# W_tok loaded first by casting loads, and the order of all queues replayed from a table

## The chip, the core and the metric

The kernel runs on one core of a Trainium2 chip. The core has four engines that compute: TensorE (PE; its weight loads are listed apart as PEld), VectorE (DVE), ScalarE (ACT) and GpSimd (POOL). Each works through its own queue of instructions in order, and semaphores tie the queues together. SyncE (SP) only issues data transfers (DMAs); POOL issues some as well. All DMAs share 16 DMA engines. The metric is the time of one execution on the device, in microseconds (us).

## The reference

Inputs are q, k, v of shape (8 batches, 8 heads, 576, 64), a norm vector g of 64, a token-mixing matrix W_tok (576 x 576), W_ch1 (512 x 2048), W_ch2 (2048 x 512) and five vectors of 512.

```python
kv  = einsum('bhsd,bhse->bhde', k, v)           # attention without a softmax
o   = einsum('bhsd,bhde->bhse', q, kv)
x   = o / sqrt(mean(o*o, -1) + 1e-6) * g        # heads joined: (8, 576, 512)
tok = einsum('ts,bsd->btd', W_tok, alpha1 * x + beta1)
u   = x + lam * tok
ch  = relu((alpha2 * u + beta2) @ W_ch1) @ W_ch2
out = u + lam * ch
```

## The kernel before, in words

The 576 tokens of a batch are four chunks of 128 and a tail of 64; the tails of an even and an odd batch share one tile of 128 rows. For each batch the stages are:

- **kv** (L749, L755; for batch 0 `kv_first`, L725): the products of k and v, in f32.
- **norm** (L843; for batch 0 `norm_half`, L864): q times kv, then the mean square by an ACT square (L807) and a DVE reduction (L810), a square root (L813), a reciprocal (L816), and products that give x (L828) and r, which is x scaled for the token mix (L831).
- **tok** (L914; for batch 0 `tok_half`, L929; tails L948): W_tok transposed times r, five matmuls to a group, the fifth over the tail of 64 tokens. beta1's part enters through this fifth chunk: the tile wt holds, beside W_tok's last 64 rows, rows with W_tok's row sums (`wsums`, L1103 to L1113), which meet lam * beta1 in the tile rtl. DVE adds the result to x (L921; L937 for batch 0).
- **a2**: alpha2 * u + beta2 in bf16 and transposed. Batch 0 does it with TensorE transposes (`a2_pair`, L968) and ACT copies (L972). The others use two POOL operations per chunk (L986, L989) and a transposing DMA (L993).
- **ch1** and **ch2** (L1002, L1031; tails L1014): the channel mix, bf16 matmuls of 512 columns, with relu on ACT (L997). Then lam times the result (L1058), the addition (L1063) and the store.

The first channel-mix matmul of batch 0 (L1002) ends what is called the head below. In the head, batch 0 is done in two halves of the heads (j = 0, 1): pairs of heads of q, k and v are loaded by SP (`load_pair`, L611), q is rearranged by POOL (L698) and transposed by TensorE in f32 (`qt_early`, L703), and so on to a2. W_tok is loaded by SP in f32 (L629, L631), transposed by TensorE in f32 (L1081, L1084) and copied to bf16 by ACT (L1087, L1092). "Fillers" are matmuls on a constant tile (L597) whose results nobody uses. The weights W_ch1 and W_ch2 are loaded by POOL with a cast to bf16 (L1163, L1169), k and v of later batches also by POOL (L1186, L1190), q of later batches by SP in pieces of 128 bytes (L1178).

The order of the work is not that of the Python text. Every operation is recorded with what it reads and writes (`Prog.op`, `dma`, `mm`); `schedule` then plays the recorded operations through estimated costs, due times (`t0`, `pace`), shifts of single operations (`shift`) and extra waits (`gate`), puts out one sequence, and chooses the PSUM banks. A unit of that sequence is one operation or two TensorE operations woven together, matmul by matmul. Where TensorE has nothing to do in the head, `schedule` puts in fillers.

Of the kernel before, what the change touches and what calls it, by code (L numbers as in the profile page):

```python
# [9 lines left out]
BF16 = mybir.dt.bfloat16  # L10
# [8 lines left out]
DM = 512  # L19
# [4 lines left out]

class Op:


    __slots__ = ("bias", "q", "kind", "cost", "lat", "fns", "pri", "idx", "deps", "raw", "alloc",
                 "tiles", "start", "end", "pos", "waits", "inc", "clock", "slot", "nbytes",
                 "val", "margin", "tag", "narrow", "urgent", "ns")  # L30

    def __init__(self, q, kind, cost, lat, fns, pri, idx):
        self.q, self.kind, self.cost, self.lat = q, kind, cost, lat
        self.fns, self.pri, self.idx = fns, pri, idx
        self.deps, self.raw = set(), set()
        self.alloc, self.tiles = [], []
        self.start = self.end = self.pos = None
        self.waits, self.inc, self.clock = [], False, None
        self.slot = self.nbytes = self.val = self.ns = None
        self.margin = 0.0  # L40
        self.tag, self.narrow, self.urgent = "", False, False
# [12 lines left out]
class Prog:  # L54
    ENGINES = ("PE", "ACT", "DVE", "POOL")

    def __init__(self, nc, stack):
# [7 lines left out]
        self.main, self.fill = [], []  # L65
        self.bias = 0.0
        self.reach = 24
        self.warm, self.began, self.early, self.lead = 6.0, False, 45.0, 100.0
        self.t0, self.pace, self.last, self.shift = 31.0, 1.28, None, {}
        self.gate = {}  # L70
# [4 lines left out]
    def _add(self, o, r, w, after):  # L75
# [10 lines left out]
        for key in w:  # L86
# [5 lines left out]
            for y in self.readers.get(key, ()):  # L92
                if y is not o:
                    o.deps.add(y)
                    if not isinstance(key, Bank) and key[0] == "sm":
                        o.raw.add(y)
# [11 lines left out]
    def op(self, q, cost, fn, r=(), w=(), pri=0.0, lat=0.15, after=()):  # L108
        o = Op(q, "c", cost, lat, [fn], self.bias + pri, len(self.ops))
        o.bias = self.bias  # L110
        return self._add(o, r, w, after)

    def dma(self, q, slot, nbytes, fn, r=(), w=(), pri=0.0, after=(), issue=0.55):
        o = Op(q, "d", issue, 0.0, [fn], self.bias + pri, len(self.ops))
        o.slot = slot
        o.nbytes, o.ns = nbytes if isinstance(nbytes, tuple) else (nbytes, 20.0)
        o.bias = self.bias
        return self._add(o, r, w, after)

    def mm(self, stream, cols, fns, r=(), w=(), slow=False, after=(), margin=0.3,  # L120
           urgent=False):

        n = len(fns)
        per = cols * MM_NS + 0.0025
        each = slow if isinstance(slow, float) else {"r": 0.213}.get(slow, 0.109)
        o = Op("PE", "w" if slow and each is not slow else "m",
               n * (max(per, each) if slow else max(per, 0.056)),
               0.24, fns, self.bias, len(self.ops))
        o.bias = self.bias
        o.margin, o.narrow, o.urgent = 0.0 if urgent else margin, cols < 512, urgent  # L130
        (self.main if stream == "main" else self.fill).append(o)
        return self._add(o, r, w, after)


    def schedule(self):
        for i, j in self.gate.items():
            self.ops[i].deps.add(self.ops[j])
        due, t = {}, self.t0
# [1195 lines left out]
```

## Time and profile before

| | us |
|---|---|
| three runs | 354.62, 355.60, 358.28 |
| median | 355.60 |
| span of the profiled execution | 354.8 |
| TensorE busy | 341.3 |
| VectorE busy | 189.8 |
| GpSimd busy | 161.4 |
| ScalarE busy | 149.0 |

The span runs from the first to the last instruction of the profiled execution; the page gives no other time of that execution, so the span is used as its time. It lies between the runs' lowest time and their median. TensorE's matmuls are pipelined: the time from the start of one to the start of the next says more than the length of one. In rows of the timeline the first two numbers are the start and the length in us; in rows of groups the number behind the count is the total busy time, the next the mean in ns, then the idle time before them and what ended it.

### The profile page before, as it was taken

Reading aid. Unit: us, or ns where it says so; the run is one execution under the profiler, and the core shown is the slowest. Engines: PE = TensorE matmul, PEld = TensorE weight load, DVE = VectorE, ACT = ScalarE, POOL = GpSimd, SP = SyncE. Lnnn points to the kernel's source line nnn. Section 1 sums busy time; section 2 is a strip of 40 time slices with the busy share of each in tenths; the row PEclk is TensorE's granted clock in tenths of the full one; section 3 lists DMA queues with packets and bytes.
Section 4 is the critical chain, followed back from the end, with each engine's and each line's share of the span. In section 5 each row is a group of like instructions: output and inputs, shape, how many; then the busy total and the mean of one; then the engine's idle time right before and its main releaser. Section 6 shows DMA issues by size and latency. Waiting matters only on the chain.

```text
span 354.8 us, 5512 instructions
## 1 busy us (share of the span) xinstructions
PE 341.3 (96%) x2208; PEld 198.4 (56%) x2241; DVE 189.8 (54%) x343; ACT 149.0 (42%) x291; POOL 161.4 (45%) x151
## 2 busy tenths in 40 slices
PE   4979999999999999999999999999999999999994
PEld 3858964454664664466556545564476444444644
DVE  3475778204685579636745676459444963210043
ACT  3335397004940386126823366136552273026400
POOL 2397410965308940985058612973192306930000
PEclk9989999999999999999999999999999999999999
DMA  7999899969598399138963995239922110330012
GB/s 241 267 336 161 139 251 230 144 110 198 120 262 134 90 232 213 31 93 195 247 61 76 221 173 124 46 116 258 175 33 89 59 31 15 75 105 0 2 69 79
DMA packets 107952, 48.76 MB, mean 137 GB/s; under 512 B 81997, under 2 KB 99925, under 8 KB 107928
## 3 DMA queue, kind: packets, MB, share of 16 engines
q1 hardware_dynamic: 82312, 27.71, 42.9%
q0 software_dynamic: 25616, 20.71, 34.0%
q8 instruction: 17, 0.28, 0.3%
q14 instruction: 7, 0.06, 0.1%
HBM read 38.82 MB, written 9.44 MB: 136 GB/s over the span
## 4 chain that ended last, share of the span: by engine, by line
PE 87%; DMA 5%; SPq 2%; POOL 2%; DVE 1%; issue 1%; ACT 0%; DVEq 0%; POOLq 0%
PE ps L1031 31%; PE ps L1002 31%; PE ps L914 8%; PE ps L1014 4%; PE ps L843 3%; DMA hh<-in_moe_w_tok_dram 2%; PE ps L749 2%; DMA w<-in_k_dram 2%; PE ps L597 1%; SPq L611 1%; PE ps L929 1%; POOL a1f L986 1%; PE ps L948 1%; PE ps L1081 1%; PE ps L1042 1%; DMA lam_bc<-in_moe_lam_dram 1%
## 5 line engine op out<-in xcount | busy, mean ns | idle before, releaser
L1031 PE MATMUL ps<-w,hh 128*128 128x512 bf16 x543 | 135.3, 383 | 0.7 <-issue 0.3
L1002 PE MATMUL ps<-a2m,w 128*128 128x512 bf16 x501 | 117.8, 381 | 1.0 <-DVE tmp L1058 0.4
L997 ACT ACTIVATE hh<-ps 128x512 bf16<-128x512 f32 x144 | 84.8, 597 | 64.3 <-PE ps L1002 54.9
L1031 PEld LDWEIGHTS ps<-w,hh 128*128 128x128 bf16 x560 | 52.9, 97 | 58.8 <-issue 1.6
L1002 PEld LDWEIGHTS ps<-a2m,w 128*128 128x128 bf16 x512 | 48.7, 98 | 56.5 <-DVE tmp L1058 1.3
L986 POOL TENSOR_TENSOR a1f<-xm,a_bc 128x512 f32<-128x512 f32 x28 | 35.5, 1273 | 68.6 <-DVE xm L921 68.3
L1058 DVE TENSOR_TENSOR tmp<-ps,lam_bc 128x512 f32<-128x512 f32 (+2 forms) x38 | 25.1, 661 | 69.8 <-PE ps L1031 56.5
L1063 POOL TENSOR_TENSOR xm<-xm,tmp 128x512 f32<-128x512 f32 x28 | 35.4, 1269 | 34.7 <-DVE tmp L1058 34.7
L810 DVE TENSOR_REDUCE small<-sq 128x8 f32<-128x512 f32 (+2 forms) x41 | 27.2, 666 | 25.2 <-ACT sq L807 25.0
L989 POOL TENSOR_TENSOR a2b<-a1f,b_bc 128x512 bf16<-128x512 f32 x32 | 40.3, 1273 | 0.7
L843 PE MATMUL ps<-kvc,qt 128*128 128x128 f32 x140 | 40.1, 395 | 0.0
L921 DVE TENSOR_TENSOR xm<-ps,xm 128x512 f32<-128x512 f32 x28 | 19.3, 690 | 29.8 <-PE ps L914 28.5
L749 PE MATMUL ps<-vr,kr 128*128 128x128 f32 x112 | 32.3, 395 | 0.0
L807 ACT ACTIVATE sq<-ps 128x512 f32<-128x512 f32 (+2 forms) x41 | 23.9, 584 | 19.3 <-PE ps L843 18.5
L1199 ACT ACTIVATE qt<-qp 128x576 fp32r<-128x576 f32 x24 | 15.9, 682 | 32.3 <-DVE qp L1196 32.3
L843 PEld LDWEIGHTS ps<-kvc,qt 128*128 128x128 f32 x140 | 27.4, 199 | 2.0
L914 PE MATMUL ps<-rm,wt 128*128 128x512 bf16 x109 | 28.3, 379 | 0.2
L597 PE MATMUL ps<-fil 128*128 128x128 bf16 x109 | 20.0, 245 | 4.5 <-DVE fil L596 4.5
L819 DVE TENSOR_TENSOR ps<-ps,small 128x512 f32<-128x512 f32 (+1 forms) x35 | 23.5, 690 | 0.5
L766 ACT ACTIVATE kvo<-ps 64x256 f32<-64x256 f32 x14 | 5.3, 378 | 43.0 <-PE ps L755 42.8
L749 PEld LDWEIGHTS ps<-vr,kr 128*128 128x128 f32 x112 | 22.3, 201 | 0.9
L1196 DVE STREAM_TRANSPOSE qp<-qs 128x576 f32<-128x576 f32 x24 | 17.3, 755 | 5.6 <-DMA qs<-in_q_dram 3.4
(109 smaller groups left out, 324.0 us busy)
## 6 DMA issues: line engine op xcount, KB each, us to landing
out_dram<-xm SPq DMA_DIRECT2D x32, 256.0 KB, 2.3
kr<-in_k_dram POOLq DMA_DIRECT2D x7, 1024.0 KB, 9.0
vr<-in_v_dram POOLq DMA_DIRECT2D x7, 1024.0 KB, 11.4
qs<-in_q_dram SPq DMA_DIRECT2D x24, 288.0 KB, 11.1
w<-in_moe_w_ch_dram POOLq DMA_DIRECT2D x3, 1024.0 KB, 10.2
xm<-in_q_dram SPq DMA_DIRECT2D x8, 288.0 KB, 4.4
w<-in_k_dram SPq DMA_DIRECT2D x4, 288.0 KB, 5.6
qs<-in_v_dram SPq DMA_DIRECT2D x4, 288.0 KB, 5.9
```

The costliest lines, as they stand in the source:

```text
L749: P.mm("fill", 128, [lambda e, t=t, c=c, h=h, o=128 * (h % 4): e.matmul(t.ap()[:, o:o + 128], kr4[:, h, c:c + 2, :].rearrange("p c d -> p ...
L807: P.op("ACT", act(n), lambda e: e.activation(sq[rs, s3, 0:nst, :].rearrange("p h e -> p (h e)"), ps(), ACT.Square), r=[t], w=[("sq", s3)])
L810: P.op("DVE", dve(n), lambda e: e.tensor_reduce(out=st, in_=sq[rs, s3, 0:nst, :], axis=AX.X, op=ALU.add), r=[("sq", s3)], w=[("sm", s4)])
L843: P.mm("fill", 128, [lambda e, p=p: e.matmul(dst(p), qt[:, p, cs], kvc[:, i, p, :], start=(p == 0), stop=(p == 3)) for p in range(4)], r=[ ...
L914: P.mm("fill", 512, [lambda e, sc=sc: e.matmul(t.ap(), wt[:, sc if sc < 4 else tw(b), 128 * c:128 * c + 128], rsrc(b, sc, al), start=(sc = ...
L986: P.op("POOL", pool(512), lambda e: e.tensor_tensor(out=a1f[:, s], in0=x, in1=a2_bc[:], op=ALU.mult), r=ks + ["a2"], w=[("a1f", s)])
L989: P.op("POOL", pool(512), lambda e: e.tensor_tensor(out=a2b[:, c], in0=a1f[:, s], in1=b2_bc[:], op=ALU.add), r=[("a1f", s), "b2"], w=[("a2 ...
L997: P.op("ACT", act(512), lambda e: e.activation(dst, t.ap(), ACT.Relu), r=[t], w=keys, pri=-1000)
L1002: P.mm("main", 512, [lambda e, dj=dj: e.matmul(t.ap(), w1[:, dj, 128 * fj:128 * fj + 128], a2m[:, b % 3, dj, :], start=(dj == 0), stop=(dj ...
L1031: P.mm("main", 512, [lambda e, fj=fj, t=t, c=c: e.matmul(t.ap(), (ht[:, fj, 128 * c:128 * c + 128] if c < 4 else hl[:, fj, :]), w2[:, fj, ...
L1058: P.op("DVE", dve(z - a), lambda e: e.tensor_tensor(out=tmp[:, s, a:z], in0=t.ap()[:, 0:z - a], in1=lam_bc[:, a:z], op=ALU.mult), r=[t, "l ...
L1063: lambda e: e.tensor_tensor(out=x, in0=x, in1=tmp[:, s, a:z], op=ALU.add),
```

## The change

Three things change.

- **W_tok.** It is loaded by POOL's queue in three loads that cast to bf16 (chunks 0 and 1, chunks 2 and 3, the tail of 64 rows), and is transposed by ordinary bf16 matmuls against a bf16 identity matrix, one operation per block.
- **Waits.** In batch 0's token mix the first four chunks are an operation of their own; only the operation with the fifth chunk waits for the row sums and rtl. The row sums of the columns 512 to 576 have a key of their own.
- **Order.** `schedule` is gone. `replay` reads the whole sequence from a table, ORDER. A word is the number of an operation, in the order in which operations are recorded; numbers behind colons are its PSUM banks; a + weaves operations (now also one with two others); `~26` means 26 fillers. GATES adds waits: `11: 8` lets operation 11 wait for 8 as well.

Numbers that the text below uses: 24, 22 and 23 are W_tok's loads (tail, chunks 0 and 1, chunks 2 and 3); 88 to 112 W_tok's transposes; 50, 51, 134 and 135 the four k/v products of batch 0; 8 and 9 the first loads of k and v, 11 the second v, 16 the third q; 166 the last token-mix addition that the first two a2 transposes read; 303 the first channel-mix matmuls; 184 the first load of W_ch1, 89 the copy of W_tok's chunk 0.

```diff
+ORDER = """
+0 9 28 24 ~26 8 201 14 3 27 22 10 30 6 33 31 4 5 1 200 2 29 32 23 88:1 94 100 106 112 50:2:3 11
+115 114 16 13 119:4 12 7 96:5 120 97 102:6 103 121 18 84:7 85 108:1 109 90:4 26 91 ~33 15 19 20
+42 17 188 104 86 87 110 105 98 99 89 111 92 93 51 113 ~24 95 126 55 54 34 52 101 107 194 53
+116:7 43 192 35 46:1 117 44:3 184 40 47 118 48:4 134:5:6 25 45 36 190 21 58:2 37 ~4 49 189 59
+68:1 193 38 187 76:7 69 60:3 39 191 77 186 70 56:4 61 127 78 71 ~3 79 57 128:2 80 62 130:4 81 72
+124:7 82 131 ~7 73 129 212 125 132:4 135 63 74 133 ~7 136 139 137 138 64 156:1 65 140:7 75 157
+148:2 158 141 ~17 66 142 149 159 150 143 220 167:4 144 151 145 219 168 152 146 164:5 67 160 153
+221:6 211 165 154 223:3 147 225:7 161 177:2 169 162 217:1 155 174:4 166 218 178 175 83 179 170:5
+172:1 185 176 171 215:2 224 180:4 173 195 182:5 222 181 303:0 196 226 301:3 183 213:1 307 305
...
+GATES = {7: 9, 8: 0, 11: 8, 13: 14, 15: 31, 16: 9, 18: 0, 19: 32, 20: 8, 23: 29, 24: 0, 38: 11, 39:
+    17, 40: 114, 41: 315, 122: 125, 123: 122, 184: 89, 186: 42, 187: 95, 190: 31, 191: 11, 192:
...
-    def schedule(self):
...
+    def replay(self, order, gates):
+
+        for i, j in gates.items():
             self.ops[i].deps.add(self.ops[j])
...
+        for word in order.split():
+            if word[0] == "~":
+                self.sequence.append((self.idler(int(word[1:])),))
+                continue
+            unit = []
+            for part in word.split("+"):
+                at, *banks = part.split(":")
+                o = self.ops[int(at)]
+                for tile, b in zip(o.alloc, banks):
+                    tile.bank = int(b)
+                    if owner[tile.bank] is not None:
+                        o.deps.update(owner[tile.bank].ops)
+                    owner[tile.bank] = tile
+                unit.append(o)
+            self.sequence.append(tuple(unit))
...
+        P.op("DVE", dve(128), lambda e: e.tensor_copy(out=idb[:], in_=ident[:]), r=["ident"],
+             w=["idb"])
...
-        P.dma("SP", "wl", dcost(512, 92), lambda e: e.dma_start(
-            wl, moe_w_tok[0:512, :].rearrange("(c p) s -> p c s", p=128)), w=["wl"])
-        P.dma("SP", "wlt", dcost(64, 220), lambda e: e.dma_start(
-            wlt, moe_w_tok[512:576, :]), w=["wlt"])
+        for c in (0, 2):
+            P.dma("POOL", "wl%d" % c, dcost(256, 98), lambda e, c=c: e.dma_start(
+                wl[:, c:c + 2, :], moe_w_tok[128 * c:128 * c + 256, :].rearrange(
+                    "(c p) s -> p c s", p=128)), w=[("wl", c), ("wl", c + 1)], issue=0.9)
+        P.dma("POOL", "wlt", dcost(64, 150), lambda e: e.dma_start(
+            wlt, moe_w_tok[512:576, :]), w=["wlt"], issue=0.8)
...
-            for c in range(2 * ch, 2 * ch + 2):
+            cc = range(2 * ch, 2 * ch + 2)
+            for scs in (range(4), (4,)):
                 P.mm("fill", 256, [lambda e, sc=sc, c=c: e.matmul(
                     t.ap()[:, 256 * (c % 2):256 * (c % 2) + 256],
                     wt[:, sc, 128 * c:128 * c + 128],
...
+                    r=[rk(0, sc, p) for sc in scs for p in (2 * j, 2 * j + 1)] +
+                    [("wt", sc) for sc in scs] + (lb(0) + [("ws", 4)] if 4 in scs else []),
+                    w=[t])
...
-            P.mm("fill", 128, [lambda e, tc=tc: e.transpose(
-                t.ap(slice(0, n))[:, 128 * tc:128 * tc + 128], wl[:, tc, cols], ident[:])
-                for tc in range(4)], r=["ident", "wl"], w=[t], slow=True)
...
+            for tc in range(4):
+                P.mm("fill", 128, [lambda e, tc=tc: e.matmul(
+                    t.ap(slice(0, n))[:, 128 * tc:128 * tc + 128], wl[:, tc, cols], idb[:],
+                    start=True, stop=True)], r=["idb", ("wl", tc)], w=[t])
...
-        P.schedule()
+        P.replay(ORDER, GATES)
         P.synchronize()
         P.emit()
```

350 lines of the change are left out of this document (54 added, 296 removed), and 85 rows, old and new, of tables (GATES, ORDER, cs).

## The prediction

> **What bounds the kernel now.** I read the page, then busy times cut at the first and last channel-mix matmul, the chain of waits of the head, and the engines' timelines there.
>
> ```profile
> span 354.8 us, 5512 instructions
> PE 341.3 (96%) x2208; PEld 198.4 (56%) x2241; DVE 189.8 (54%) x343; ACT 149.0 (42%) x291; POOL 161.4 (45%) x151
> core 0: us, PE busy (x) PEld busy (x) DVE busy (x) ACT busy (x) POOL busy (x), PEclk, DMA share, GB/s
> 0.00:44.37 44.37, 37.20 (x421) 31.73 (x423) 24.76 (x55) 16.94 (x40) 22.89 (x31) 0.96 1.01 229
> 44.37:350.69 306.32, 304.15 (x1788) 166.72 (x1818) 164.77 (x288) 132.04 (x252) 138.52 (x120) 1.00 0.75 125
> 350.69:354.80 4.11, 0.00 (x0) 0.00 (x0) 0.28 (x1) 0.00 (x0) 0.00 (x0) 1.00 0.25 62
> ```
>
> From 44.37 TensorE is idle for 2.2 of 306.3 us at full clock: only less matmul work shortens that stretch, and the change removes none. What can shrink is the 44.4 us before it.
>
> ```profile
> 0.90 0.48 DVE L1232 MEMSET kr<- 64x512 f32 x1 [0.90 <-PEq L1319]
> 4.29 0.17 DVE L596 MEMSET fil<- 128x128 bf16 x1
> 4.52 1.03 PE L597 MATMUL ps<-fil 128*128 128x128 bf16 x8 [4.52 <-DVE fil L596]
> 16.27 1.07 POOL L1186 DMA_DIRECT2D kr<-in_k_dram  x1 [3.83 <-DMA qs<-in_v_dram]
> 15.58 8.33 DMA hh<-in_moe_w_tok_dram
> 15.50 1.26 PE L725 MATMUL ps<-qs,w 64*64 64x64 f32 x36
> 16.90 1.26 PE L725 MATMUL ps<-qs,w 64*64 64x64 f32 x36
> 23.95 0.33 PE L1081 MATMUL ps<-ident,hh 128*128 128x128 f32 x1 [1.96 <-DMA hh<-in_moe_w_tok_dram]
> 44.37 0.38 PE L1002 MATMUL ps<-a2m,w 128*128 128x512 bf16 x1
> ```
>
> In the head the last product of k and v (L725) is over at 18.1. What follows waits 8.33 us for W_tok, which is queued behind twelve q, k, v loads; its transposes begin at 23.95, and the first channel-mix matmul, F below, stands at 44.37.
>
> **The change, part by part.** The span is F, plus the rest (354.8 - 44.4 = 310.4), plus what the new order adds to or takes from the rest.
>
> *TensorE's way to the last k/v product.* W_tok (words 24, 22, 23 of the table) goes first on POOL's queue. Its 25 transposes (88 to 93) are bf16 matmuls, without the interleaved fillers. TensorE still starts with a filler, and the memset of its operand (0.17) was the tenth on VectorE, at 4.29; in the table it is the first, so TensorE starts at 0.90 + 0.17 and a hand-over, about 1.2, not at 4.52.
>
> ```profile
> 20.87 1.12 PE L678 MATMUL ps<-a2m,one 1*128 1x512 f32 x2
> 33.46 0.67 PE L597 MATMUL ps<-fil 128*128 128x128 bf16 x9
> 33.97 0.28 PE L703 MATMUL ps<-ident,xm 128*128 128x128 f32 x1
> 44.59 1.04 PE L968 MATMUL ps<-ident,xm 128*128 128x128 f32 x8
> 45.46 0.59 PE L1002 MATMUL ps<-a2m,w 128*128 128x512 bf16 x2
> ```
>
> Start to start these give 0.056 us for a warm filler (9 in 0.51) and 0.109 for an f32 transpose (8 in 0.87); at 4.52 eight cold fillers took about 0.12 each. Ahead of the end of the last k/v product (135) the table holds 26 cold fillers (3.1), 71 warm ones (4.0), 30 small bf16 matmuls for W_tok and its sums (2.0 with the cold ones), four k/v products (1.2 each, the first about 0.6 more cold: 5.4), five 512-wide sums (1.1), 18 transposes (2.0), 10 f32 norm matmuls (1.0) and three small broadcasts (1.4, from 1.12 for the larger). That is 20.0; from 1.2 it ends at 21.2, and I add 1.0 for waits that the fillers don't cover: 22.2. As a check by loads: the last v load had landed by 16.27. W_tok adds 0.65 MB of bf16 ahead of it.
>
> ```profile
> kr<-in_k_dram POOLq DMA_DIRECT2D x7, 1024.0 KB, 9.0
> w<-in_moe_w_ch_dram POOLq DMA_DIRECT2D x2, 512.0 KB, 5.5
> w<-in_moe_w_ch_dram POOLq DMA_DIRECT2D x3, 1024.0 KB, 10.2
> ```
>
> Those casting loads grow by 4.7 us for 512 KB more, so W_tok as one stream is worth at most 6.0 and, where it shares engines with q, k, v (DMA share 1.01 above), perhaps half. The last v lands at about 19 (17 to 22), its product ends 1.3 later: TensorE's own queue ends last, or nearly. Extra waits in the table (v of pair 1 for k of pair 0, q of pair 2 for v of pair 0) hold SP while two loads are still moving; I cost them at nothing, and 1 us each if that cover is gone.
>
> *From there to F.* VectorE's queue decides. Behind the last k/v copies it has, up to the addition that the first two a2 transposes need (166): two reductions of 512 and one of 256, four reciprocals, three 512 scalings and one of 256, three r products (two 512, one 256), two additions, and two copies.
>
> ```profile
> L810 DVE TENSOR_REDUCE small<-sq 128x8 f32<-128x512 f32 x32 | 21.7, 679 | 13.4 <-ACT sq L807 13.3
> L816 DVE RECIPROCAL small<-small 128x8 f32<-128x8 f32 x32 | 5.7, 190 | 4.4 <-ACT small L813 4.4
> L828 DVE TENSOR_TENSOR xm<-ps,small 128x512 f32<-128x512 f32 x4 | 2.7, 687 | 0.1
> L828 DVE TENSOR_TENSOR xt<-ps,small 64x256 f32<-64x256 f32 x2 | 0.8, 416 | 0.1
> L831 DVE TENSOR_TENSOR rm<-xm,e_bc 128x512 bf16<-128x512 f32 x2 | 1.9, 944 | 0.0
> L937 DVE TENSOR_TENSOR xm<-ps,xm 128x512 f32<-128x512 f32 x4 | 2.8, 688 | 1.0 <-PE ps L929 0.9
> L972 ACT ACTIVATE a2m<-ps,ab 128x512 bf16<-128x512 f32 x4 | 3.1, 774 | 0.8 <-PE ps L968 0.8
> ```
>
> Nine full-width passes at 0.69 (6.2; r taken at 0.69 too), three half ones at 0.42 (1.3), four reciprocals (0.8) and two copies, by the nearest row 0.2 each, come to 8.6. Then four transposes (0.44 and 0.2 of latency), two ACT copies of 0.77 and hand-overs: 2.5. F = 22.2 + 8.6 + 2.5 = 33.3. Lower bound 31 (no uncovered wait), upper 38 (r at 0.94 or more, last v at 22, one cold spell). Against 44.4: -11.1.
>
> A wait can cost more than itself here.
>
> ```profile
> 20.80:24.20 3.40, 1.44 (x7) 0.53 (x6) 2.43 (x6) 1.57 (x4) 2.71 (x4) 1.00 1.21 347
> 24.20:27.60 3.40, 3.40 (x24) 2.71 (x23) 1.60 (x2) 0.59 (x1) 2.74 (x3) 0.50 1.78 364
> ```
>
> A stretch with 1.96 us of idling and 1.44 busy was followed by 3.4 us at half clock, some 1.7 us lost. One such spell stands in the upper bound. [...]
>
> *What moves behind F.* The first 24 f32 matmuls for batch 1 (20 of kv, 4 of norm) stood ahead of F and stand after it in the table.
>
> ```profile
> 47.57 0.39 PE L1002 MATMUL ps<-a2m,w 128*128 128x512 bf16 x1
> 47.60 0.63 PE L843 MATMUL ps<-kvc,qt 128*128 128x128 f32 x3
> 48.08 3.66 PE L1002 MATMUL ps<-a2m,w 128*128 128x512 bf16 x15
> 51.64 0.39 PE L1002 MATMUL ps<-a2m,w 128*128 128x512 bf16 x1
> 51.68 0.41 PE L843 MATMUL ps<-kvc,qt 128*128 128x128 f32 x1
> 51.93 0.39 PE L1002 MATMUL ps<-a2m,w 128*128 128x512 bf16 x1
> ```
>
> A bf16 matmul of 512 takes 0.216. One woven f32 matmul adds 0.075 (0.29 from 51.64 to 51.93), three in a row add 0.098 each. 24 cost 1.8 to 2.4; four transposes fewer behind F give 0.4 back: +1.9. Weaving one f32 matmul among two groups of bf16 ones, not one, changes neither rate: nothing. The tail ends on a 256-wide block where it ended on 128: two DVE operations, +0.3.
>
> *Batch 0's token mix.* Only its fifth chunk waits for the row sums now. But in the table the sums are done some 10 us ahead of that mix: nothing by itself.
>
> *Weights.* w1's first load waits for the copy of W_tok's chunk 0; behind it in POOL's queue stand the other w1 loads and k and v of batch 1. Issued from about 13 on, at 4.7 per 512 KB of cast output, w1's first part lands by about 20 with the short k, v tails ahead of it, the second (1 MB) by 30, wanted at 33 and 34.7; k and v of batch 1 follow at half that price (no cast; 9.0 from issue to landing includes the queue) by 37, at worst 43, wanted at 40. I cost this at nothing; without the cover it is up to 3.
>
> *The rest, replayed.* Between the end of the first token-mix group and the first channel-mix matmul of a batch, TensorE's work in the table is 13.4 us for batch 1 and 12.3 for batch 2 (18.8 and 14.5 before); for batches 3 to 7 it is 17 to 21.
>
> ```profile
> L986 POOL TENSOR_TENSOR a1f<-xm,a_bc 128x512 f32<-128x512 f32 x28 | 35.5, 1273 | 68.6 <-DVE xm L921 68.3
> a2m<-a2b SPq DMA_TRANSPOSE x28, 2.5
> ```
>
> In that time POOL has eight 1.27 us operations (10.2), after an addition (0.69), before a transposing DMA (2.5): 13.6 with hand-overs. So batch 1 waits 0.2 to 3 us, batch 2 about 1.3 to 3: I take +2.0 for both, 0 to 6 as the ends.
>
> Sum: 33.3 + 310.4 + 1.9 + 0.3 + 2.0 = 347.9, against the profiled span of 354.8, which stands 0.8 under the median of 355.6 and 0.2 over the fastest run. I give **348**.
>
> **The rivals.** *Slower: W_tok holds TensorE.* In the table the transposes of W_tok's first four blocks stand ahead of the second k/v product (51). The order is fixed, so what lands late there delays all behind it, us for us. I assume that the second block lands by 10.3. If POOL's three loads went one after the other at 5.5 each from 2.0, it lands at 18.5: +8.2, and a cold spell 1.7: 358. From a landing at about 16 on the change is a loss against the median. For it: the loads start amid DVE's memsets and twelve other loads. Against: 5.5 is mostly latency and a larger load. [...]
>
> *Given back in the rest.* Waits of 3 us at batches 1 and 2 and one of 2 at the weights, with F at 34: 354. For it: the slack counted above is at or under the need. Against: before, 14.5 sufficed.
>
> *The change does only half of what it says.* W_tok first costs q, k, v what it gains, F stays near 40 because the VectorE chain stretches beside POOL (r once took 0.94 on average where 0.69 is usual): 354 to 355.
>
> *More.* No wait at batches 1 and 2 and F at 31: 343.5.
>
> **How the numbers follow.** Forecast (345 to 351): 0.55. More: 0.12. Given back: 0.10. Half: 0.09. Slower by W_tok or a like wait: 0.14. A range from 343 to 356.5 leaves out about 2 in 10. Under 1% (3.6 us) a measurement of this kernel can't tell a change, its own runs spread by that much. Faster by over 1% (under 352.0): forecast, more and a part of given back, 0.71; within 1%: 0.16; slower: 0.13.
>
> **What would show it.** In the changed profile: first filler near 1.2; last k/v product over near 22; first channel-mix matmul at 33.3 (31 to 38); from there some 312 us to the last matmul's end and the tail, with waits of 1 to 3 us only at the starts of batches 1 and 2. The forecast is wrong if W_tok's second block lands after 13, if F is past 38, or if TensorE idles over 5 us after F.

## The result, and the profile after

The changed kernel takes 372.06 us (median; 370.17 to 374.15) against 355.15 for the kernel before (354.62 to 358.28): a ratio of 1.047, interval 1.040 to 1.054. It is slower by 17 us, where 348 was forecast. In the runs below, the kernel before gave medians of 355.1 to 356.2 beside them, and each ratio is to the one that stood beside it.

The page of the changed kernel, then its busy times in stretches cut at its own first channel-mix matmul (42.57) and the end of its last matmul (365.90), and in two stretches of the time that are needed further on. Columns as in the same view of before: length; busy time and count of TensorE, its weight loads, VectorE, ScalarE, GpSimd; granted clock; DMA share; GB/s.

```profile
span 371.6 us, 5530 instructions
PE 348.3 (94%) x2216; PEld 200.3 (54%) x2253; DVE 190.4 (51%) x344; ACT 143.3 (39%) x291; POOL 163.4 (44%) x154
```

```profile
0.00:42.57 42.57, 36.21 (x412) 30.43 (x415) 22.89 (x52) 16.09 (x38) 24.59 (x34) 0.92 1.00 229
42.57:365.90 323.33, 312.10 (x1804) 169.85 (x1838) 166.66 (x290) 127.16 (x254) 138.80 (x120) 0.99 0.68 118
365.90:371.60 5.70, 0.00 (x0) 0.00 (x0) 0.85 (x2) 0.00 (x0) 0.00 (x0) 0.71 0.21 57
45.00:62.00 17.00, 16.95 (x100) 10.22 (x101) 7.93 (x17) 12.47 (x27) 0.00 (x0) 1.00 0.78 149
62.00:85.00 23.00, 20.93 (x105) 10.25 (x106) 11.42 (x19) 0.69 (x2) 14.43 (x14) 1.00 1.05 164
```

In the kernel before, the last matmul ends at 350.32; the cut at 350.69 that stands further up lies 0.4 us behind it. Cut alike:

```profile
44.37:350.32 305.95, 304.15 (x1788) 166.72 (x1818) 164.47 (x286) 132.04 (x252) 138.52 (x120) 1.00 0.75 125
350.32:354.80 4.48, 0.00 (x0) 0.00 (x0) 0.58 (x2) 0.00 (x0) 0.00 (x0) 1.00 0.23 59
```

The head became 1.8 us shorter (42.57 against 44.37), not 11; three runs below with the same order up to there have its end at 44.01, 43.60 and 42.80 (experiments 1, 3 and 5), so that of the 1.8 as little as 0.4 may be left. The stretch behind it became 17.4 us longer (323.33 against 305.95), the tail 1.2 (5.70 against 4.48). TensorE stood idle for 11.2 of those 323.33 us, where it was 1.8 of 305.95. The two stretches of time that are needed further on, in the kernel before:

```profile
45.00:62.00 17.00, 16.86 (x90) 9.17 (x90) 14.44 (x26) 13.83 (x27) 2.15 (x3) 1.00 1.15 243
62.00:85.00 23.00, 22.57 (x120) 11.36 (x122) 6.57 (x11) 2.37 (x5) 17.70 (x16) 1.00 0.93 133
```

From 45 to 62 us VectorE was busy for 14.4 us before and for 7.9 after, and GpSimd not at all. TensorE looks the same in both (16.9), so that its share tells nothing; it worked at other things there, and what VectorE should have done, the norms of batch 1, came later.

TensorE's timeline at the places that matter (start, length, line, operation, what ended the idle time before it):

```profile
1.05 2.21 PE L444 MATMUL ps<-fil 128*128 128x128 bf16 x19 [1.05 <-DVE fil L443]
12.98 1.18 PE L938 MATMUL ps<-idb,hh 128*128 128x128 bf16 x10 [0.82 <-DMA hh<-in_moe_w_tok_dram]
26.86 1.29 PE L576 MATMUL ps<-qs,w 64*64 64x64 f32 x36
36.20 1.05 PE L782 MATMUL ps<-rm,wt 128*128 128x256 bf16 x8 [1.96 <-DVE rm L682]
42.57 0.81 PE L858 MATMUL ps<-a2m,w 128*128 128x512 bf16 x3
66.93 1.04 PE L766 MATMUL ps<-rm,wt 128*128 128x512 bf16 x4 [0.94 <-DVE rtl L674]
84.90 0.99 PE L858 MATMUL ps<-a2m,w 128*128 128x512 bf16 x2 [1.07 <-DMA a2m<-a2b]
214.42 1.66 PE L858 MATMUL ps<-a2m,w 128*128 128x512 bf16 x4 [4.68 <-DMA a2m<-a2b]
```

The last k/v product (the row at 26.86) is over at 28.1, forecast 22.2; it was over at 18.1 before, when W_tok came behind it. The longest wait behind the head is at 214.42, in batch 4. A milestone for each batch is ScalarE's first relu (us):

| | batch 0 | 1 | 2 | 3 | 4 | 5 | 6 | 7 | last TensorE end |
|---|---|---|---|---|---|---|---|---|---|
| before | 49.2 | 82.8 | 125.5 | 162.0 | 204.6 | 240.9 | 282.9 | 316.5 | 350.3 |
| after | 45.2 | 86.9 | 131.2 | 167.0 | 218.1 | 256.1 | 294.8 | 330.6 | 365.9 |

From the head's end to batch 1's relu it is 44.3 us against 38.4 (+5.9); from there to the last TensorE end 279.0 against 267.5 (+11.5), of which batch 3 to batch 4 alone gives 51.1 against 42.6 (+8.5). With the head (-1.8) and the tail (+1.2) that is the 16.8 by which the spans differ.

**Batch 1's chain.** Its products of k and v, the k/v copies, and the additions of its token mix, before and then after (behind the count the shortest, the median and the longest in ns, then when the first and the last one start, then the shape):

```profile
L749 PE MATMUL ps<-vr,kr x16: 304/307/308, 35.8 to 39.8; 128*128 128x128 f32 x16
L768 DVE TENSOR_TENSOR kvc<-ps,kvo x2: 415/421/427, 41.4 to 41.9; 64x256 fp32r<-64x256 f32 x2
L921 DVE TENSOR_TENSOR xm<-ps,xm x4: 690/691/692, 61.8 to 68.8; 128x512 f32<-128x512 f32 x4
```

```profile
L600 PE MATMUL ps<-vr,kr x16: 273/276/412, 48.9 to 50.7; 128*128 128x128 f32 x16
L619 DVE TENSOR_TENSOR kvc<-ps,kvo x2: 416/422/428, 52.4 to 52.8; 64x256 fp32r<-64x256 f32 x2
L773 DVE TENSOR_TENSOR xm<-ps,xm x4: 681/692/692, 68.2 to 73.2; 128x512 f32<-128x512 f32 x4
```

k and v of batch 1 are ready for the norms 11 us later than before (52.8 against 41.9). Their loads come later too. GpSimd's queue after, and issue to landing of the same load of k (the last number, us), before and after:

```profile
16.86 0.70 POOL L1048 DMA_DIRECT2D vr<-in_v_dram  x1 [4.95 <-DVE a2m L506]
18.83 1.51 POOL L1021 DMA_DIRECT2D w<-in_moe_w_ch_dram  x2
21.21 0.90 POOL L1044 DMA_DIRECT2D kr<-in_k_dram  x1
```

```profile
kr<-in_k_dram POOLq DMA_DIRECT2D x1, 1024.0 KB, 11.6
```

```profile
kr<-in_k_dram POOLq DMA_DIRECT2D x1, 1024.0 KB, 18.0
```

Behind two loads of W_ch1 and the load of v, k is issued at 21.2 and lands at 39.3; before it was issued at 16.3 and landed at 27.8. Ahead of all of them GpSimd's queue stood for 4.95 us: the short tail of v, the first of these rows, has an extra wait in the table, for a product on VectorE. With k landing at 39.3 its products couldn't have stood where before has them (35.8); but they start only at 48.9, so that most of the lateness is in the order.

### The profile page after: what moved, and what is told of

Same layout as the page of the kernel before. It is cut to its first block, busy times and chain, and to the rows that moved or that the text cites. A ratio compares the mean times of both kernels' runs of the same rounds, so it can differ in the third digit from the quotient of the medians.

```text
span 371.6 us, 5530 instructions
## 1 busy us (share of the span) xinstructions
PE 348.3 (94%) x2216; PEld 200.3 (54%) x2253; DVE 190.4 (51%) x344; ACT 143.3 (39%) x291; POOL 163.4 (44%) x154
## 4 chain that ended last, share of the span: by engine, by line
PE 65%; DVE 12%; POOL 8%; DMA 6%; ACT 4%; issue 2%; SPq 2%; DVEq 0%; POOLq 0%
PE ps L858 23%; PE ps L887 21%; PE ps L766 6%; PE ps L870 4%; DMA a2m<-a2b 4%; POOL a1f L842 3%; POOL a2b L845 3%; DMA hh<-in_moe_w_tok_dram 2%; DVE ps L670 2%; PE ps L694 2%; DVE rm L674 2%; ACT hh L853 2%; PE ps L600 2%; SPq L849 1%; DVE small L661 1%
## 5 line engine op out<-in xcount | busy, mean ns | idle before, releaser
L858 PE MATMUL ps<-a2m,w 128*128 128x512 bf16 x497 | 125.1, 388 | 7.4 <-DMA a2m<-a2b 6.6
L853 ACT ACTIVATE hh<-ps 128x512 bf16<-128x512 f32 x144 | 79.9, 596 | 114.4 <-PE ps L858 84.2
L858 PEld LDWEIGHTS ps<-a2m,w 128*128 128x128 bf16 x512 | 43.7, 99 | 54.3 <-DMA a2m<-a2b 7.5
L887 PEld LDWEIGHTS ps<-w,hh 128*128 128x128 bf16 x560 | 43.7, 98 | 42.7 <-ACT hh L853 0.9
L694 PE MATMUL ps<-kvc,qt 128*128 128x128 f32 x140 | 52.9, 404 | 0.1
L661 DVE TENSOR_REDUCE small<-sq 128x8 f32<-128x512 f32 (+2 forms) x41 | 26.9, 665 | 28.2 <-ACT sq L658 28.1
L600 PE MATMUL ps<-vr,kr 128*128 128x128 f32 x112 | 40.2, 385 | 0.0
L766 PE MATMUL ps<-rm,wt 128*128 128x512 bf16 x110 | 29.5, 381 | 2.6 <-DVE rm L674 1.6
L600 PEld LDWEIGHTS ps<-vr,kr 128*128 128x128 f32 x112 | 20.2, 191 | 11.5 <-issue 1.5
L870 PEld LDWEIGHTS ps<-a2l,w 128*128 128x128 bf16 x256 | 16.9, 98 | 7.2
L870 PE MATMUL ps<-a2l,w 128*128 128x128 bf16 x256 | 19.5, 219 | 0.1
## 6 DMA issues: line engine op xcount, KB each, us to landing
kr<-in_k_dram POOLq DMA_DIRECT2D x7, 1024.0 KB, 10.1
w<-in_moe_w_ch_dram POOLq DMA_DIRECT2D x3, 1024.0 KB, 13.3
```

Source lines behind the costliest of these rows:

```text
L600: P.mm("fill", 128, [lambda e, t=t, c=c, h=h, o=128 * (h % 4): e.matmul(t.ap()[:, o:o + 128], kr4[:, h, c:c + 2, :].rearrange("p c d -> p ...
L661: P.op("DVE", dve(n), lambda e: e.tensor_reduce(out=st, in_=sq[rs, s3, 0:nst, :], axis=AX.X, op=ALU.add), r=[("sq", s3)], w=[("sm", s4)])
L694: P.mm("fill", 128, [lambda e, p=p: e.matmul(dst(p), qt[:, p, cs], kvc[:, i, p, :], start=(p == 0), stop=(p == 3)) for p in range(4)], r=[ ...
L766: P.mm("fill", 512, [lambda e, sc=sc: e.matmul(t.ap(), wt[:, sc if sc < 4 else tw(b), 128 * c:128 * c + 128], rsrc(b, sc, al), start=(sc = ...
L853: P.op("ACT", act(512), lambda e: e.activation(dst, t.ap(), ACT.Relu), r=[t], w=keys, pri=-1000)
L858: P.mm("main", 512, [lambda e, dj=dj: e.matmul(t.ap(), w1[:, dj, 128 * fj:128 * fj + 128], a2m[:, b % 3, dj, :], start=(dj == 0), stop=(dj ...
```

## The experiments

In the order tables 303 to 300 are the first channel-mix matmuls, 202 to 206 the k and v products of batch 1, 243, 267, 235, 251, 259 its norms, 213 to 225 (odd) its q transposes, 191 and 193 the loads of its k and v, 192 and 194 their short tails, 184 and 190 the loads of W_ch1 that are issued first. All kernels compute the whole result. Times from F to the last matmul are to that matmul's start: 305.7 in before, 323.1 in after.

**1. Which half of the order costs? After's head with before's order behind it.** From the first channel-mix matmul on, the table holds what the kernel before puts out, numbers shifted by 17.

```diff
-222 181 303:0 196 226 301:3 183 213:1 307 305 ...
+222 181 183 163 122 123 41 198 199 300:0 301:1 213:6 214 216 226 202:4+302:3 204:5+303:2 205+304 ...
```

> The changed program with its own order up to the first channel-mix matmul of batch 0 (F), and from there the order of the kernel before; the 24 f32 matmuls that stood ahead of F there are woven in right behind it. Theory 'order of the rest': F stays at 42.6, F to the last TensorE start falls from 323.1 to 306 to 309 (305.7 before, plus 1.9 for the 24 matmuls), tail 4.7: 354 to 357. Rival 'head': what the head leaves behind (k and v of batch 1 at 39, w1 and w2 late, the split token mix) is what costs the 17 us behind F; then it stays above 365.

Measured: 363.88, ratio 1.022 (1.018 to 1.026). 8 us of the 17 go, 8 stay, and those stand before batch 1's relu (91.1 against 82.8); from there each batch is 8.2 to 8.3 behind, to batch 7. With the products of k and v woven in right behind F (44.01), where before has them ahead of it, TensorE waits three times for VectorE (0.51, 0.92, 3.26 us), longest in the norms:

```profile
58.37 0.33 PE L691 MATMUL ps<-kvc,qt 128*128 128x128 f32 x1 [3.26 <-DVE xm L673]
```

**2. The other half: before's program and head, after's order behind F** (numbers shifted back by 17).

```diff
-        P.schedule()
+        P.replay(ORDER, GATES)
```

> The program of before (W_tok in f32, late, token mix not split) with its own order up to F, and from there the order of the changed kernel. Theory 'order of the rest': F 44.4, then some 321 (323.1 less 1.9 for the 24 f32 matmuls done ahead of F) and a tail of 6: 369 to 373, with a wait of 4 to 5 us at the start of batch 4. Rival 'head': 355 to 359.

Measured: 375.23, ratio 1.053 (1.047 to 1.058). Its head is that of before (44.73), and from there to the last matmul it takes 323.5, as after does (323.1). So the order behind the head is enough to lose it all, without W_tok's new way; little of it (a wait of 1.23 at 47.42) is for weights, which before's head loads later than this order asks. The two longest waits:

```profile
66.66 1.04 PE L897 MATMUL ps<-w,hh 128*128 128x512 bf16 x4 [3.28 <-DVE rm L689]
216.92 1.04 PE L868 MATMUL ps<-a2m,w 128*128 128x512 bf16 x4 [3.24 <-DMA a2m<-a2b]
```

Batch 1's k/v copies are done at 41.7 here, as early as in before (42.3), and still its token mix starts adding at 74.8 (61.8 in before). Since 1 takes 8 off and 2 adds 19, the two halves don't add up: both make batch 1's norms late, and one lateness hides the other. No run has W_tok's new way alone, with the planner of before.

**3. Batch 4's stall: two loads of q for batch 6 moved behind the transposing DMAs 770 and 760 in SP's queue.**

```diff
-886 769 884 888 898 905:3+843+858 827 770 906 760 844
+769 884 898 905:3+843+858 827 770 906 760 886 888 844
```

> The changed kernel with one edit: two of the q loads of batch 6 are issued behind the transposing DMAs of batch 4 in SP's queue instead of between them. Theory 'SP's queue': the wait of 4.7 us at 214 goes and with it the half-clock spell behind it (1.7): 372 less 6.4 = 365.7, within 1.5. Rival 'the transposes are slow whatever stands before them' (7.5 us beside the v load on POOL's queue): over 370.

Measured: 367.18, ratio 1.031 (1.025 to 1.037): 4.9 us for two words. SP's queue in after, then here:

```profile
200.81 2.83 SPq L1036 DMA_DIRECT2D qs<-in_q_dram  x2
204.09 4.07 SPq L849 DMA_TRANSPOSE a2m<-a2b  x2
```

```profile
197.37 6.42 SPq L849 DMA_TRANSPOSE a2m<-a2b  x3
204.24 8.76 SPq L1036 DMA_DIRECT2D qs<-in_q_dram  x3
```

The chain of waits of after has the transposing DMA behind the two loads:

```profile
204.09 2.75 SPq L849
206.90 7.48 DMA a2m<-a2b
```

It took 7.48 us to land, where 2.5 is the median of all 28 before. With the loads behind, TensorE doesn't wait at batch 4, and from batch 3's relu to batch 4's it is 44.7 us, not 51.1.

How the two loads make it late, this run doesn't tell apart. In after the last transposing DMA is issued (206.90) behind a load of v on GpSimd's queue (1 MB, landed at 214.13), and lands just after it, at 214.37:

```profile
205.60 0.89 POOL L1044 DMA_DIRECT2D vr<-in_v_dram  x1 [2.67 <-ACT sq L658]
```

Here it is issued ahead of that load (202.53 against 204.63) and lands in 2.89 us; in 10, with the same edit, too (4.87 us). In experiment 6 the two loads of q stand ahead of it as in after, yet it is issued ahead of the load of v (206.18 against 206.94) and lands in 3.39 us, and TensorE doesn't wait at batch 4. In 2, 4 and 8, as in after, it comes behind the load of v, and takes 6.3 to 6.6 us. In after the transposing DMA ahead of it, whose issue took 2.75 us from 204.09 on and so reached past that of the load of v, is late too: it takes 9.7 us to land. So in these runs the last one took 6.3 to 7.5 us where it was issued behind the load of v, and 2.9 to 4.9 where it was issued ahead of it; no run moves the load of v alone.

**4. Three small moves in the head:** the last v load of batch 0 (21) earlier in SP's queue, GpSimd's copy of a q pair (43) and the second k/v product (51) earlier, ahead of W_tok's second block.

```diff
-17 188 104 ... 93 51 113 ~24 ... 53 116:7 43 ... 190 21 58:2
+17 21 188 51 ... 53 43 104 ... 93 113 ~24 ... 116:7 ... 190 58:2
```

> The changed kernel with three moves in its table, all in the head: the last v load ahead of the first DMA into rtl in SP's queue, the second k/v product ahead of the transposes of W_tok's second block, the copy of the second q pair ahead of the v tail load in POOL's queue. Theory 'queues stand behind waits': the last k/v product ends at 22 to 24 instead of 28.1, F falls from 42.6 to 37 to 39, and the time to 366 to 368. Rival 'VectorE or the weights bound the head': the last k/v product falls but F stays over 41 and the time over 370.

Measured: 372.61, ratio 1.047 (1.042 to 1.051): nothing, a miss. The last v load lands at 18.2 (22.1 in after), but the last k/v product starts at 27.00 (26.86 in after; 27.06 to 28.30 in other runs with after's order of the head). The earlier loads didn't help here, where TensorE's own order was as long as that.

**5. Experiment 1 with batch 1's norms set 2 to 6 groups later and its second token-mix group 2 later.**

```diff
-... 243:6+310 ... 267:7+312 ... 235:4+314 ... 251:5+316:0
+... 243:6+316:0 ... 267:7+318:1 ... 235:4+322:2 ... 251:5+326:1
```

> As the run with the changed head and the order of before behind F, but the five norm matmul groups of batch 1 are woven two to six channel-mix groups later and its token mix stands two later, so that TensorE doesn't wait for the k/v chain of VectorE (4.7 us of waits from 46 to 58 there, and half clock after them). Theory 'order of the rest': F at 42.6 to 44, F to the last start 306 to 309, tail 4.7: 354 to 357. Rival 'the 24 late f32 matmuls and the split token mix cost more than 2 us behind F': 359 or more, without idle gaps.

Measured: 362.82, ratio 1.022 (1.015 to 1.029): a miss, forecast 354 to 357. The one wait of 3.26 became two, 1.74 for the norms (`xm L673`) and 1.80 for r (`rm L671`), so batch 1's relu comes at 88.5, 2.6 earlier than in 1, of which 1.2 is F (42.80 against 44.01 with the same order of the head); from there on the kernel is as fast as before. Later places on TensorE didn't mend this: VectorE gets its work too late.

**6 and 7. The head rewritten for an early last product** (fillers cut, loads and products brought forward), with after's rest (6) and with that of 5 (7).

```diff
-~33 15 19 20 42 17 188 104 ...
+42 126 43 15 19 20 17 21 188 ~14 51 52 ... 104 ...
```

> The changed kernel with the order of its head written anew, from the transposes of W_tok's first block to the last norm group of batch 0: the second k/v product, W_tok's second block, the q transposes, then the products and norms as their loads land; 62 fillers of this stretch become 39, the row sums go ahead of the last product, the last v load ahead of the rtl DMAs, the q copy ahead of the v tail load. Theory 'TensorE's fixed order, with fillers and row sums, holds the head': the last k/v product ends at 23 to 24 instead of 28.1, F falls from 42.6 to 37 to 39, the time from 372 to 366 to 368. Rival 'VectorE and GpSimd hold F': the last product is early but F stays over 41 and the time over 370.

> The head written anew and the order of before behind F, both. If both theories hold, their gains add: 355 to 356 less 4 to 5, so 350 to 352, faster than both kernels. If the rest can't use an earlier F (k of batch 1 lands at 39, the second part of w1 and w2 at 44 to 56), TensorE waits for weights between 40 and 60 and it ends at 354 to 356.

Measured: 371.62 (1.047) and 365.56 (1.029, 1.023 to 1.036): misses. The last product starts at 27.55, no earlier, and the first channel-mix matmul at 45.69, later. With the fillers cut, the 36 matmuls of the second product took 2.19 us, where the last one's take 1.26, as those of the second do in after (14.09): a spell of half clock, by my estimate from these times.

```profile
13.38 2.19 PE L576 MATMUL ps<-qs,w 64*64 64x64 f32 x36
```

That 6 takes no longer than after, with F 3.1 later, is luck of another place: batch 4's stall is missing in it (see 3).

**8. Is VectorE slowed by GpSimd?** In after the two r products of batch 0 (L682) take twice the 0.69 that I had taken; GpSimd runs beside them:

```profile
32.03 1.27 POOL L684 TENSOR_TENSOR xm<-xm,g_bc 128x512 f32<-128x512 f32 x1
32.47 1.39 DVE L682 TENSOR_TENSOR rm<-xm,e_bc 128x512 bf16<-128x512 f32 x1
34.55 1.60 DVE L682 TENSOR_TENSOR rm<-xm,e_bc 128x512 bf16<-128x512 f32 x1
```

Here four of GpSimd's operations stand behind VectorE's 154, by their place and a wait.

```diff
-... 67 160 153 221:6 211 165 154 ... 147 ... 155
+... 160 153 221:6 165 154 67 211 147 155          (GATES + 67: 154)
```

> The changed kernel with four GpSimd operations of 32 to 37.5 us (g products and the copy of a q pair) waiting until VectorE's second r product is done, so that nothing of GpSimd runs beside the two r products that took 1.39 and 1.60 us. Theory 'GpSimd beside it doubles the r product': both take 0.68 to 0.72, the wait of TensorE ahead of the second half of the token mix falls from 1.96 to 0.5 or less; the four operations then end later, so F changes by -1 to +1. Rival 'the product is slow by its form (f32 in, bf16 out, broadcast)': 1.4 to 1.6 as before.

Measured: one time, 373.35; the profile is what counts:

```profile
33.76 0.69 DVE L683 TENSOR_TENSOR rm<-xm,e_bc 128x512 bf16<-128x512 f32 x1
```

This product and the other (at 35.14) are back at 0.69 each, 1.6 us less together; GpSimd was idle for the 2.56 us ahead of 35.91, so that nothing of it ran beside them. F stands at 42.82, but the last k/v product started 1.1 later here (28.00): from its start to F it is 14.8 us, against 15.5 to 15.7 in after and in 1, 3 and 5. So some 0.8 of the 1.6 is gained, in one profile; the rest goes where GpSimd's moved work is waited for later (waits of 1.19 and 0.68, where after has 1.96).

**9 and 10. k and v of batch 1 loaded ahead of W_ch1, their products ahead of F,** with before's order behind (9) and with after's own and the move of 3 (10).

```diff
-... 126 55 ... 43 192 ... 193 38 187 ... 39 191 77 ...
+... 126 43 193 191 55 ...
-... 202:6 325 41 203 333 198 204:1 ...     (behind 303)
+... 185 195 202:6 204:1 167:4 ...          (ahead of 300 to 303)
```

> The changed head with batch 1's v and k loads (2 MB) ahead of w1's first part in GpSimd's queue, the last v load of batch 0 ahead of the rtl DMAs, and the twenty f32 products of batch 1's k and v ahead of F in the place of fillers and of the 1.96 us wait; behind F the order of the kernel before, unshifted. Theory 'batch 1's chain': in the changed kernel k of batch 1 lands at 39.3 (31.1 before) and its k/v chain ends at 53.3 (42.3 before), and with the order of before behind F that is what still cost 7 us (first channel mix of batch 1 at 88.5 instead of 82.8). With it early: k lands by 28, the chain ends by 43, F 42.5 to 44, first channel mix of batch 1 at 81 to 83, the time 353 to 356. Rival 'the rest is longer by the changed head's other traces (w1, w2 late, split token mix)': 359 or more, with waits for weights behind F.

> The same head, with the changed kernel's own order behind F, only the two q loads of batch 6 behind batch 4's transposing DMAs as in the run that tried this alone. Theory 'batch 1's chain and SP's queue are most of it': 367 of that run less 3 to 5 (waits of 0.9 and 0.5 to 1.1 at batch 1, 2 us of f32 products moved ahead of F): 362 to 364. If the order behind F costs by itself whatever feeds it: 366 to 368.

Measured: 371.76 (1.047) and 373.28 (1.050). The load did come early, but the table gave those products a PSUM bank that batch 0's tail norm still held:

```profile
36.38 0.90 PE L597 MATMUL ps<-vr,kr 128*128 128x128 f32 x3 [6.26 <-DVE xt L676]
```

That wait of 6.26 us was my table's, and the times of these two runs settle little. (The 31.1 that the expectation gives for k in before is the landing of v; k landed at 27.8.) But F is at 53.8 in both, and from there to the last matmul it is 310.9 in 9 and 312.1 in 10. With batch 1's products done early and SP's queue mended, after's own order is thus only 1.2 longer than before's order in 9, though an F this late may hide other waits.

**11. As 9, with the products in free banks,** the q transposes of batch 1 behind F, and the norms woven from group 306 on.

```diff
-202:6 204:1 167:4 168 ...
+202:5 204:6 205 167:4 168 ...
```

> The run with batch 1's k and v first, mended: there TensorE stood 6.3 us at 30.1, because the first k/v product wrote the PSUM bank that the norm of batch 0's tail still held; here the products take the two banks of batch 0's last k/v products, the q copies of batch 1 follow behind F, and its norms and token mix lie one group later than before. Theory 'batch 1's chain' (k landing, k/v product, five norms on VectorE, token mix, GpSimd): chain ready by 41 (53.3 in the changed kernel), first channel mix of batch 1 at 83 to 85 (86.9 there, 82.8 before), the time 354 to 358. Rival 'the changed head's other traces make the rest longer': over 360, with waits for weights.

Measured: 357.55, ratio 1.0038 (1.001 to 1.0065), as forecast. Against 5, which has much the same order behind batch 1, 5.3 us less, with F about where 5 has it (42.80); of the three edits none was tried alone. F stands at 42.22, batch 1's relu at 84.2 (88.5 in 5), F to the last matmul takes 309.2. One wait is left behind F that is over 1 us, again for VectorE at the token mix:

```profile
62.96 1.04 PE L763 MATMUL ps<-rm,wt 128*128 128x512 bf16 x4 [1.19 <-DVE rm L671]
```

**12. VectorE's six q copies of batch 1 given to ScalarE** (`qt_early`), with the q transposes of batch 1 back ahead of F and its norms from F on.

```diff
-                if b:
-                    P.op("DVE", dve(128 * n) + 0.08, lambda e, dst=dst, src=src: e.tensor_copy(
-                        out=dst, in_=src()), r=[t], w=keys)
-                else:
-                    P.op("ACT", ...
+                P.op("ACT", act(128 * n) + 0.08, lambda e, dst=dst, src=src: e.activation(
+                    dst, src(), ACT.Identity), r=[t], w=keys)
```

> The same, with one edit of the program: the six copies of batch 1's transposed q (3.4 us) go from VectorE to ScalarE, which in the changed kernel idles 8.9 us ahead of 40.8, and so ahead of F; the norms of batch 1 start right at F. Theory 'VectorE is the queue that both batches stand in from 28 to 60': the token mix of batch 1 starts 2 to 3 us earlier than in the run beside it, and the time is 2 to 3 us less: 351 to 355, at or under the kernel before. Rival 'ScalarE then holds the relus, or TensorE the head': no gain, or up to 2 us more.

Measured: 355.58, ratio 1.0004 (0.9976 to 1.0032). From F (43.35) to the last matmul 305.0, with no wait over 0.25 us after F; 0.7 us less than before's 305.7.

**13. As 12, with the head rewritten:** second k/v product ahead of W_tok's second block, fewer fillers, W_tok's row sums behind the last norm.

```diff
-~33 15 19 20 42 17 21 188 104 86 87 110 ... 93 51 113 ~24 ... 116:7 ... 134:5:6 ...
+15 19 20 17 21 42 188 34 35 ~14 36 40 51 37 126 25 189 ~8 ... 104 86 ... ~14 ... 134:5:6 ... 148:2 158 141 75 116:3 ...
```

> The run with ScalarE copies, and its head from W_tok's first block on written anew: the second k/v product ahead of W_tok's second block, the q transposes, the third product, norms and the last product following without fillers but for 34 matmuls of them ahead of waits, the row sums behind the last norm. Theory 'TensorE's fixed order holds the last k/v product, and now an earlier F can be used': that product ends at 22 to 24 (27 to 28 in the run beside it), F at 40 to 41.5 (43.4), first channel mix of batch 1 at 78.5 to 80 (81.2), the time 352.5 to 354.5, faster than both kernels by some 0.5 to 1%. Rival 'loads and the half clock hold the head' (the rewritten head alone had F at 45.7 with stretches at half clock): F at 43 or later, no gain.

Measured: 352.93, ratio 0.992 (0.990 to 0.995): faster than both kernels, 0.8% faster than the one before.

```profile
22.10 1.26 PE L569 MATMUL ps<-qs,w 64*64 64x64 f32 x36
40.61 1.04 PE L851 MATMUL ps<-a2m,w 128*128 128x512 bf16 x4
```

```profile
45.00:62.00 17.00, 16.76 (x85) 8.07 (x83) 13.16 (x23) 10.32 (x22) 5.69 (x7) 1.00 1.30 238
```

The last product is over at 23.4, F comes at 40.6, 2.7 earlier than in 12, and batch 1's relu 2.7 earlier too (78.5 against 81.2): here a gain of the head is kept us for us. VectorE is busy for 13.2 of the 17 us from 45 on, near the 14.4 of before, and GpSimd has begun.

**14. The copies of 12 alone, in the kernel before** (whose planner then lays the order anew). The edit is that of 12.

> The kernel before with only the six q copies of batch 1 moved from VectorE to ScalarE. Theory 'the token-mix weights first bring nothing by themselves, VectorE's queue does': faster than before by 1 to 3 us, like the run with the changed head and this edit, or better. Rival 'the changed head is what lets this edit pay': within 1 us of before.

Measured: 359.49, ratio 1.010 (1.007 to 1.013). The copies alone are no gain; what 12 and 13 gain isn't just these. Whether the copies or the planner's other order cost the 1% isn't told apart.

## Why the prediction was wrong, step by step

The forecast span was 347.9, the profiled one 371.6. Of the 23.7 between them, 9.3 lie ahead of F and 14.4 behind it, where 18.6 were added and I had summed 4.2.

**"TensorE's way to the last k/v product": 22.2, measured 28.1.** The first filler was right (1.05). By 28.07 TensorE is busy for 23.9 us, where I summed 20.0, and idle for 4.2, where I allowed 1.2 at the start and 1.0 of waits: 1.83 and 0.82 of it are waits for W_tok's loads (the first at 5.84).

```profile
0.00:28.07 28.07, 23.86 (x308) 19.56 (x309) 10.17 (x28) 11.66 (x27) 12.94 (x23) 0.94 0.92 231
```

With overlaps cut, the 97 fillers take 7.8 us (7.1 summed), W_tok's matmuls and its sums 4.7 (3.1), the 18 transposes 3.1 (2.0), the four products 5.5 (5.4). Some 1.7 of the 3.9 too few is a stretch at half clock (23.54 to 26.95, shown at the end; 0.06 of 28.07 by the mean clock); the rest lies in short matmuls, which I took at the rates of long warm rows. W_tok's second block landed at 12.9, not by 10.3, but just under the 13 that I had set as a limit; that 5.5 us for a load "is mostly latency" didn't follow from my rows (10.2 less 5.5 for 512 KB more leaves 0.8), and W_tok's loads took 4.4 us from issue to landing for 72 KB, 6.8 and 8.2 for 288 KB; the rival "W_tok holds TensorE" (16 and more) didn't come. Of the extra waits that I cost at nothing, the one for k of pair 0 held SP for 1.5 us. A longer one I had not seen at all: the small DMA into rtl waits for a product on VectorE, and held SP for 7.9 us. The last v load, behind it, was issued at 18.4 and landed at 22.1 (forecast 17 to 22). The view of waits, by line and what it waited for (total, times, longest in us):

```profile
SPq L522 <- DVE a2m L509: 7.9, 1, 7.9
```

Experiment 4, where that load comes earlier and the product doesn't, shows that this was not the term that decided. Experiment 13 shows that the order of TensorE's own work was: rearranged, with the same W_tok and with the last v load where 12 has it, it ends its last product at 23.4, near my 22.2 (28.1 in 12).

**"From there to F": 11.1, measured 14.5.** VectorE's chain up to the second addition took 10.3, not 8.6; the r products at 1.39 and 1.60 are 1.6 of the 1.7, though taking that away brought F only some 0.8 nearer (experiment 8). I had 0.94 in my upper bound and took 0.69. The rest, 4.2 and not 2.5, lies on TensorE: after the wait of 1.96 at 36.20 its next stretch ran at half clock, as the step "A wait can cost more than itself" had it and my sum did not.

```profile
33.79:37.20 3.41, 1.45 (x15) 1.13 (x13) 3.38 (x7) 0.00 (x0) 2.78 (x3) 1.00 1.85 343
37.20:40.61 3.41, 3.41 (x19) 2.73 (x18) 2.52 (x5) 0.00 (x0) 3.41 (x5) 0.50 0.36 30
```

Together F is at 42.6, not 33.3: 9.3 of the 11.1 forecast were not there. The rival "half" named the stretched VectorE chain and F near 40.

**"What moves behind F": +1.9.** I counted 24 matmuls, and not what hangs on them. The products of k and v are the first link of batch 1's chain (copies, five norms on VectorE, token mix, eight GpSimd operations, transposing DMA), and the chain started 11 us later. From F to batch 1's relu it is 5.9 more, and an earlier F alone would not have helped. In 1 and 5, with before's order behind the head, the late products go with a loss of 7 to 8 us; 11, which has them ahead of F, loses 0.4%. They are not the only cause: in 2 the products are as early as in before, and with after's order behind F batch 1 comes late all the same. How the 5.9 divide between the two isn't told apart.

**"Weights": nothing.** I let k and v of batch 1 land "by 37, at worst 43, wanted at 40". k landed at 39.3, and the half price that I gave these loads no run shows: 1 MB of k took 10.1 us from issue to landing in the median, of v 8.5, 1 MB of cast weights 13.3. "Wanted" was the wrong word, since the table itself asks for it only at 48.9, and before had it by 35.8. W_ch1's first part landed at 27.3 and its second at 32.9, not by 20 and 30: their issue began at 18.8, not 13, behind the 4.95 us for which GpSimd's queue stood. The wait that I looked for wasn't there; the lateness was built into the order.

**"The rest, replayed": +2.0, with waits "only at the starts of batches 1 and 2".** At batch 1 the waits came (0.94 and 1.07), at batch 2 none. But batch 4, where I counted 17 to 21 us of cover, cost most: its last transposing DMA took 7.48 and not 2.5, where two loads of q ahead of it in SP's queue had put it behind a load of v. I had counted TensorE's work between two points and not what stands in the DMA queues between them (experiment 3: 4.9 us). From F to the end of the last matmul 17.4 were lost; idle time is 9.4 of it (11.2 less 1.8) and half clock about 3.4, from two stretches like this one, each 3.41 us at 0.50:

```profile
81.57:84.98 3.41, 2.33 (x12) 1.12 (x13) 1.98 (x3) 0.00 (x0) 0.60 (x1) 1.00 0.89 108
84.98:88.39 3.41, 3.41 (x11) 1.71 (x12) 1.29 (x2) 0.98 (x3) 3.41 (x4) 0.50 1.39 162
```

That leaves 4.6; 1.9 were forecast for moved matmuls, and some 2.7 us are open.

**Right:** the first filler, W_tok's landing (barely), "only less matmul work shortens that stretch" (12 and 13 have no wait behind F and still take 305.0), waits at batch 1, and the sign of the tail (+1.2 against +0.3). The signs that were to show me wrong did: F past 38 and more than 5 us idle behind it. None of my rivals had the mechanism. "Given back in the rest" had the place, with waits of 3 us at batches 1 and 2; the slower one stood in the head, and the loss came from the chains of batches 1 and 4.

## What to carry to other kernels

When work is moved behind the bound's starting point, follow the whole chain that hangs on it, not only the moved instructions: here 24 matmuls for 2 us opened a chain that, with the late norms behind it, cost 6. Count slack in every queue on the chain, DMA queues too, in the order in which they will issue; two loads that stood ahead of a transposing DMA, and put it behind a third load, cost 4.9 us (experiment 3). And an earlier start is worth something only where the next stage's inputs come early as well: with F at about 42.5, experiments 5 and 11 differ by 5.3 us, and with batch 1's k and v ahead a gain of 2.7 in the head (13 against 12) came through whole.

## What the runs showed of the hardware

- **Half clock in stretches of 3.41 us.** In the trace of after, TensorE's granted clock is 0.50 in four stretches ahead of the last matmul's end, each 3.41 us long, from 23.54, 37.20, 84.98 and 214.69 on. Their starts are 13.66, 47.78 and 129.71 us apart, which is 4.0, 14.0 and 38.0 times 3.41. The stretch ahead of 37.20 had 1.96 us idle (33.79, above), that ahead of 84.98 1.08 (81.57), and that ahead of 214.69 3.15; this one, with 1.59 idle, was not followed by half clock, the next stretch still ran at 1.00:

```profile
207.86:211.27 3.41, 1.82 (x9) 0.71 (x8) 3.38 (x7) 0.60 (x1) 3.20 (x3) 1.00 1.27 266
```

  So how much of a stretch was idle doesn't tell here whether the clock falls. One stretch busy throughout (20.13 to 23.54, with 1.5 us of matmuls that sum over a single row, `1*128`) was followed by half clock as well:

```profile
20.13:23.54 3.41, 3.41 (x39) 2.45 (x35) 1.42 (x3) 2.21 (x8) 2.65 (x4) 1.00 1.27 267
23.54:26.95 3.41, 3.41 (x22) 2.83 (x24) 2.13 (x6) 2.02 (x5) 1.82 (x3) 0.50 1.18 252
```

  Eight transposes that stand in this stretch (from 23.74) took 1.91 us; in experiments 1 and 3 they took 1.82 and 1.91, in 5, which has the same order of the head, 1.36. F stands at 42.80 in 5, and at 42.57, 44.01 and 43.60 in after, 1 and 3, so that whether this is part of why F differs isn't told. What makes the clock fall is open.
- **VectorE's product `rm<-xm,e_bc`** (128x512) took 0.69 us in both places where no operation of GpSimd ran beside it, and 1.39 and 1.60 where GpSimd's did (experiment 8).
- **A transposing DMA** took 2.5 us in the median of 28, but 7.48 where a 1 MB load of v on GpSimd's queue was issued 1.3 us ahead of it, and the one before it, whose issue began 1.5 us ahead of that load, took 9.7 (experiment 3).
